# The second sequence product as Strassen blocks, with the scores spread over four pieces per pair of tiles

## The chip, the cores and the metric

The kernel runs on one core of one Trainium2 chip. The metric is the device time of one execution in microseconds (us), taken as the median of several runs. In the profile the core's engines are PE (TensorE, matrix products; PEld is its weight load), DVE (VectorE), ACT (ScalarE), POOL (GpSimd) and SP (SyncE, which issues DMAs). Each engine works through its own queue in order; an instruction that waits holds up all that stands behind it on that engine.

## The reference

```
g = sigmoid((x * gate_w).sum(-1))                  # x: 2048 x 640
a = x @ dft_hid_re.T ;  b = x @ dft_hid_im.T
A = dft_seq_re @ a - dft_seq_im @ b                # dft_seq_*: 2048 x 2048
q = x @ w_q                                        # 32 heads, 2 x 128 each
s1, s2 = q1 @ k1.T, q2 @ k2.T                      # 16 + 16 scores per head
top 2 of each, the 4 sums, top 2 of those -> 2 of 256 experts, softmax weights
B = sum over heads and picks of weight * gelu(x @ u[e]) * v[e]
y = g * A + (1 - g) * B
```

Everything is fp32, and the indices of the top picks need nearly full precision in the scores.

## The kernel before

The order of the products is turned round: first x^T C^T for C = dft_seq_re, then for C = dft_seq_im, and the hidden transforms last. Every fp32 product is three fp32r matmuls (`mm3`, L114 to L116: high part times high, high times low, low times high). The operand is split by `split` (L109 and L110): ACT copies the high part, and POOL or DVE subtracts it to get the low part.

**Pieces.** A sequence product runs over pieces, 128 in all: product w (0 for re, 1 for im), chunk c of 512 columns t (4 of them), tile s of 128 rows (16). `seq_piece(n)` loads the C tile of piece n+5 (SP's queue), splits the tile of piece n+3 (ACT, and POOL for the low part) and issues `mm3` into five accumulation banks, one for each tile d of 128 of the 640 columns of x. The x tiles X[0..15] stay in SBUF, split. After 16 pieces ACT copies the five banks out (tile `po`) and they go to `pd` in DRAM.

**Work between pieces.** `at(n, f)` hangs a step f on piece n, and `follow(n)` issues it there. Pieces 0 to 30 carry the folding of w_q with the keys. Then each pair of tiles of x gets its scores over five pieces: four halves of 512 scores (`score_half`: 5 `mm3` each) and the products with u (`u_pair`), so that the scores of the 16 tiles end with piece 70.

**The Pump.** Work of DVE without a due piece is a set of generators in `bg`: `topk` (10 operations on 128x1024 for each tile of x), `gates` (for each four tiles, weights and indices), `rows` (PE transposes of these, spaced out by a clock), and `experts` (last in order). `run_bg(us)` is called after each `mm3` with the PE time that it stands for; it adds share*us to a credit and issues generator steps while the credit lasts. All that is issued stands in the engines' queues in that order.

**Experts.** For each half g of the tokens, `experts(g)` goes over 16 chunks: DVE builds one-hot tiles pt and qt (three 128x1024 operations, L494 to L496), PE multiplies them (16 small matmuls of 64 columns, L516, into one of two PSUM banks), DVE masks and sums the result into `cd` (L501 and L503). The half's `cd` goes to DRAM (`gd`), from which the final product takes it.

**Final product.** For each chunk c of 512 tokens, `prepare(c)` loads the ten [128, 512] tiles of pd and the two of the experts' sums, DVE multiplies the gate in (L597, L614, L615), ACT makes the high parts, POOL or DVE the low ones. `y_tile(c, j)` then makes the five tiles j of the output from twelve `mm3` each, against the split DFT matrices of the hidden dimension (DD) and v (xh, xl). DD and v are loaded and split on POOL during pieces 74 to 89. `prepare(0)` runs one term for each piece from piece 113 on. After chunk 1, `bg.drain()` issues what is left.

Of the kernel before, what the change touches and what calls it, by code (L numbers as in the profile page):

```python
# [8 lines left out]
F32 = mybir.dt.float32  # L9
# [19 lines left out]
NPC = 2 * NC * NT  # L29
# [5 lines left out]
FAR = -3.0e38  # L35


class Pump:
# [41 lines left out]
    def drain(self):  # L80
        while (c := self.one()) is not None:
            assert c >= 0
# [3 lines left out]
def gated_mix_kernel(ctx: ExitStack, tc: tile.TileContext, xT, xn, dreT, dimT, wsre, wsim, wq, kT, uT, vv, gw, out):  # L86
# [8 lines left out]
    def bank():  # L95
        return psum.tile([P, TC], F32, name="pc", tag="pc", bufs=5)

    def ps_s(shape=(P, TC)):
        return psum.tile(list(shape), F32, name="pss", tag="pss", bufs=2)

    def ps_t(shape, dt=F32):
        return psum.tile(shape, dt, name="pst", tag="pst", bufs=1)

    def stage(name):
        return big.tile([P, TC], F32, name=name, tag="stg", bufs=5)
# [6 lines left out]
    def mm3(o, wh, wl, ah, al, first, last):  # L112

        nc.tensor.matmul(o, wh, ah, start=first, stop=False)  # L114
        nc.tensor.matmul(o, wh, al, start=False, stop=False)  # L115
        nc.tensor.matmul(o, wl, ah, start=False, stop=last)  # L116
# [5 lines left out]
    bg = Pump()  # L122

    def run_bg(us):
        bg.run(us, 0.95 if p3 is None else 1.0)


    WU = big.tile([P, 2 * KD * (HH * E + NE)], F32R, name="WU", tag="WU")
    NW = KD * HH * E
    WH, WL = (WU[:, n * NW:(n + 1) * NW].rearrange("p (k c) -> p k c", k=KD) for n in range(2))  # L130
    UH, UL = (WU[:, 2 * NW + n * KD * NE:2 * NW + (n + 1) * KD * NE].rearrange("p (k c) -> p k c", k=KD)
              for n in range(2))
# [3 lines left out]


    pieces = [(w, c, s) for w in range(2) for c in range(NC) for s in range(NT)]
    pf, psp, X, xr = {}, {}, {}, {}

    def load_piece(n):
        if n < NPC:
            w, c, s = pieces[n]
            pf[n] = big.tile([P, TC], F32, name="wf", tag="wf", bufs=5)
            nc.sync.dma_start(pf[n], (wsre, wsim)[w][c, s])

    def split_piece(n):
        if n < NPC:
            h = big.tile([P, TC], F32R, name="wh", tag="wh", bufs=4)
            l = big.tile([P, TC], F32R, name="wl", tag="wl", bufs=4)  # L150
            split(pf.pop(n), h, l, nc.gpsimd)
            psp[n] = (h, l)
# [4 lines left out]
    def seq_piece(n):  # L157
        w, c, s = pieces[n]
        if s == 0:
            banks[:] = [bank() for _ in range(KD)]  # L160
# [3 lines left out]
        for d in range(KD):  # L164
            ds = slice(d * P, (d + 1) * P)
            mm3(banks[d], X[s][:, 0, ds], X[s][:, 1, ds], h, l, s == 0, s == NT - 1)
            if s == NT - 1:
                f = stage("po")
                nc.scalar.activation(f, banks[d], AF.Copy)  # L169
                nc.scalar.dma_start(pd[w, c, d], f)  # L170
            run_bg(0.68)


    p1_stack = ctx.enter_context(ExitStack())
    p1 = p1_stack.enter_context(tc.tile_pool(name="p1", bufs=1, reuse_waits="tile"))

# [27 lines left out]
    warm = big.tile([P, 4 * P], F16, name="warm", tag="wl", bufs=4)  # L204
# [56 lines left out]
    def w_transposes(G, k0, k1):  # L261
# [4 lines left out]
        h = WH[:, k0:k1, P * G:P * (G + 1)]  # L266
        nc.scalar.activation(h, t[:, :k1 - k0], AF.Copy)  # L267
        nc.vector.tensor_sub(WL[:, k0:k1, P * G:P * (G + 1)], t[:, :k1 - k0], h.bitcast(F32))  # L268
# [11 lines left out]
    xf, xs = {}, {}  # L280

    def load_xT(p):
        if p < NP:
            xf[p] = big.tile([P, 2, KD, P], F32, name="xf", tag="xf")
            for n in range(2):
                nc.sync.dma_start(xf[p][:, n], xT[2 * p + n])

    def split_xT(p):
        if p < NP:
            xs[p] = tuple(big.tile([P, 2, KD, P], F32R, name=t, tag=t) for t in ("xh", "xl"))  # L290
            f = xf.pop(p)
            for n in range(2):
                split(f[:, n], xs[p][0][:, n], xs[p][1][:, n], nc.gpsimd)
            load_xT(p + 1)


    then = {}

    def at(n, f, *args):
        then.setdefault(n, []).append(lambda: f(*args))  # L300

    def follow(n):
        for f in then.pop(n, ()):
            f()
# [14 lines left out]
    at(n - 8, load_xT, 0)  # L319
    for k in range(KD):  # L320
        at(n - 8 + k, load_u, k)
        at(n - 6 + k, split_u, k)
    at(n - 3, split_xT, 0)
    N0 = n + 1
# [23 lines left out]
    def score_half(i, a):  # L348
        xh, xl = (t[:, i % 2] for t in xs[i // 2])
# [5 lines left out]
        c = slice(a * TC, (a + 1) * TC)  # L355
        for k in range(KD):
            mm3(ps, xh[:, k, :], xl[:, k, :], WH[:, k, c], WL[:, k, c], k == 0, k == KD - 1)
            run_bg(0.68)
        nc.scalar.activation(scs[i].rearrange("p h e -> p (h e)")[:, c], ps, AF.Copy)  # L359
# [66 lines left out]
    def rows(b):  # L426
# [11 lines left out]
        for ib in range(NB):  # L438
            bg.space(lambda ib=ib: row_tile(ib), 4.0 if ib else 12.0)
# [15 lines left out]
    def u_pair(p):  # L455
        xh, xl = xs.pop(p)
# [6 lines left out]
        act = stage("act").rearrange("p (n t) -> p n t", n=2)  # L463
# [4 lines left out]
    for p in range(NP):  # L468
        n = N0 + 5 * p
        for a in range(4):  # L470
            at(n + 1 + a, score_half, 2 * p + a // 2, a % 2)
        at(n + 4, u_pair, p)
        at(n + 4, split_xT, p + 1)
    N1 = N0 + 5 * NP

    def experts(g):
# [7 lines left out]
        def build(c):  # L486
# [7 lines left out]
            nc.vector.tensor_tensor(pt, row(0), wt, op=OP.is_equal)  # L494
            nc.vector.tensor_tensor(qt, row(1), wt, op=OP.is_equal)
            nc.vector.tensor_tensor(pt, pt, row(2), op=OP.mult)  # L496
# [231 lines left out]
```

## Time and profile before

| what | us |
| --- | --- |
| median of 3 runs (lowest, highest) | 812.57 (810.55, 814.08) |
| the profiled execution, its own time | 812.46 |
| its span in the profile | 810.7 |
| PE busy in it | 798.8 (99%) |
| DVE busy | 471.9 (58%) |
| POOL busy | 278.4 (34%) |
| ACT busy | 248.8 (31%) |
| mean granted TensorE clock | 0.996 |

The span is the profiled part of an execution; 1.8 us lie around it. A group of the profile is named by line, engine and operation, with output and inputs; the line is often a helper's (L110 is every low part). Matmuls overlap in the array, so the mean time of one (about 390 ns for 512 columns) is longer than the distance between two starts.

### The profile page before, as it was taken

How to read it: one execution, taken by the hardware profiler on the slowest of the kernel's cores; microseconds unless marked ns; L12 is line 12 of the kernel's file. 1: busy time of each engine (PE TensorE's matmuls, PEld its weight loads, DVE VectorE, ACT ScalarE, POOL GpSimd, SP SyncE). 2: the span in 40 equal slices, each digit the busy share in tenths (PEclk: the TensorE clock that was granted, in tenths of full speed). 3: DMA queues.
4: the chain of work that ended last, by engine and by line, in shares of the span. 5: the costliest groups of instructions: out<-in, count | busy, mean ns of one | idle time of the engine just before them, and what ended most of it. 6: DMA issues, size and time to landing. Idle time of an engine off the chain costs nothing.

```text
span 810.7 us, 10711 instructions
## 1 busy us (share of the span) xinstructions
PE 798.8 (99%) x4227; PEld 636.3 (78%) x4227; DVE 471.9 (58%) x561; ACT 248.8 (31%) x388; POOL 278.4 (34%) x192
## 2 busy tenths in 40 slices
PE   8999999999999999999998999999999999999998
PEld 5676667888888888888786777777777888888886
DVE  4841001086886898687688199776679743334200
ACT  3433323331217125224513722311322332222200
POOL 5433124224414153242424595343346222212000
PEclk9999999999999999999998999999999999999999
DMA  9877995402115030233212632423443274434101
GB/s 345 313 273 262 238 329 169 145 13 98 66 46 176 6 105 21 90 98 117 86 56 76 208 121 65 131 76 120 154 133 119 79 233 145 140 116 144 66 26 40
DMA packets 56002, 106.31 MB, mean 131 GB/s; under 512 B 8208, under 2 KB 15248, under 8 KB 55696
## 3 DMA queue, kind: packets, MB, share of 16 engines
q1 hardware_dynamic: 42944, 87.92, 33.6%
q10 hardware_dynamic: 13008, 17.71, 6.1%
q8 instruction: 33, 0.54, 0.3%
q14 instruction: 17, 0.14, 0.1%
HBM read 85.67 MB, written 19.93 MB: 130 GB/s over the span
## 4 chain that ended last, share of the span: by engine, by line
PE 90%; DMA 4%; DVE 3%; ACT 2%; SPq 0%; ACTq 0%; issue 0%; DVEq 0%
PE pc L114 24%; PE pc L116 22%; PE pc L115 22%; PE pss L114 6%; PE pss L116 6%; PE pss L115 6%; PE pss L253 2%; DMA wq<-in_wq 2%; PE pss L516 1%; DMA xr<-in_xn 1%; DMA wf<-in_wsre 1%; ACT po L169 1%; ACT rows L435 1%; PE pst L265 0%; ACTq L170 0%; DVE rp L412 0%
## 5 line engine op out<-in xcount | busy, mean ns | idle before, releaser
L110 POOL TENSOR_TENSOR wl<-wf,wh 128x512 fp32r<-128x512 f32 x128 | 187.4, 1469 | 281.3 <-ACT wh L109 266.1
L114 PE MATMUL pc<-wh,X 128*128 128x512 f32 x640 | 258.2, 404 | 0.4 <-ACT X L109 0.3
L115 PE MATMUL pc<-wl,X 128*128 128x512 f32 x640 | 251.0, 392 | 0.9 <-POOL wl L110 0.9
L116 PE MATMUL pc<-wh,X 128*128 128x512 f32 x640 | 251.1, 392 | 0.5 <-DVE X L110 0.3
L114 PEld LDWEIGHTS pc<-wh,X 128*128 128x128 f32 x640 | 120.9, 189 | 35.3 <-issue 8.1
L116 PEld LDWEIGHTS pc<-wh,X 128*128 128x128 f32 x640 | 120.7, 189 | 27.4 <-DVE X L110 1.3
L115 PEld LDWEIGHTS pc<-wl,X 128*128 128x128 f32 x640 | 121.0, 189 | 24.7 <-POOL wl L110 1.7
L109 ACT ACTIVATE wh<-wf 128x512 fp32r<-128x512 f32 x128 | 81.0, 633 | 130.4 <-PE pc L116 86.3
L373 DVE TENSOR_REDUCE mm<-sc 128x64 f32<-128x1024 f32 x32 | 39.0, 1220 | 67.7 <-ACT sc L359 67.2
L114 PE MATMUL pss<-WU,xh 128*128 128x512 f32 x160 | 62.5, 391 | 0.0
L116 PE MATMUL pss<-WU,xl 128*128 128x512 f32 x160 | 62.3, 389 | 0.0
L115 PE MATMUL pss<-WU,xh 128*128 128x512 f32 x160 | 62.3, 389 | 0.0
L114 PE MATMUL pc<-pz,DD 128*128 128x512 f32 x160 | 62.3, 389 | 0.0
L116 PE MATMUL pc<-pz,DD 128*128 128x512 f32 x160 | 62.2, 389 | 0.0
L115 PE MATMUL pc<-pz,DD 128*128 128x512 f32 x160 | 62.2, 389 | 0.0
L110 POOL TENSOR_TENSOR pz<-pr,pz 128x512 fp32r<-128x512 f32 x19 | 27.1, 1427 | 98.0 <-ACT pz L109 84.7
L110 POOL TENSOR_TENSOR xl<-xf,xh 128x640 fp32r<-128x640 f32 x16 | 32.9, 2079 | 75.4 <-ACT xh L109 75.4
L359 ACT ACTIVATE sc<-pss 128x512 f32<-128x512 f32 x32 | 21.1, 658 | 113.1 <-PE pss L116 112.7
L375 DVE TENSOR_TENSOR eq<-sc,mm 128x1024 f16<-128x1024 f32 x32 | 45.8, 1430 | 1.1
L109 ACT ACTIVATE pz<-pr 128x512 fp32r<-128x512 f32 x32 | 19.9, 631 | 78.5 <-DVE pr L597 50.4
L268 DVE TENSOR_TENSOR WU<-pst,WU 128x512 fp32r<-128x512 f32 (+1 forms) x16 | 7.8, 490 | 61.8 <-ACT WU L267 61.6
L501 DVE TENSOR_TENSOR tmp<-pss,mask 128x512 f32<-128x512 f32 x32 | 22.0, 689 | 34.6 <-PE pss L516 34.5
(112 smaller groups left out, 1066.3 us busy)
## 6 DMA issues: line engine op xcount, KB each, us to landing
wq<-in_wq SPq DMA_DIRECT2D x32, 640.0 KB, 6.2
wf<-in_wsre SPq DMA_DIRECT2D x64, 256.0 KB, 5.3
wf<-in_wsim SPq DMA_DIRECT2D x64, 256.0 KB, 2.9
pd<-po ACTq DMA_DIRECT2D x40, 256.0 KB, 3.6
pr<-pd SPq DMA_DIRECT2D x40, 256.0 KB, 3.3
xr<-in_xn SPq DMA_DIRECT2D x16, 320.0 KB, 6.2
xf<-in_xT SPq DMA_DIRECT2D x16, 320.0 KB, 3.3
out_y<-yo ACTq DMA_DIRECT2D x19, 256.0 KB, 2.4
```

The lines of the kernel that those rows point to most:

```text
L109: nc.scalar.activation(h, f, AF.Copy)
L110: eng.tensor_sub(l, f, h.bitcast(F32))
L114: nc.tensor.matmul(o, wh, ah, start=first, stop=False)
L115: nc.tensor.matmul(o, wh, al, start=False, stop=False)
L116: nc.tensor.matmul(o, wl, ah, start=False, stop=last)
L169: nc.scalar.activation(f, banks[d], AF.Copy)
L253: nc.tensor.matmul(ps[32 * j:32 * j + 32, :HALF], kp[:, 8 * G // H, r, :], w[:, j], start=(r == 0), stop=(r == 1))
L359: nc.scalar.activation(scs[i].rearrange("p h e -> p (h e)")[:, c], ps, AF.Copy)
L373: nc.vector.tensor_reduce(m, sc, op=OP.max, axis=AX.X)
L375: nc.vector.tensor_tensor(eq, sc, m[:, :, None].to_broadcast([P, HH, E]), op=OP.is_equal)
L435: nc.scalar.activation(ROWS[i // 8][:, :, :, i % 8], t, AF.Copy)
L501: nc.vector.tensor_tensor(tmp, t.rearrange("p m (e t) -> p (m e) t", t=4), mask4[:, None, :].to_broadcast([P, 8 * E, 4]), op=OP.mult)
```

## The change

The first product (C = dft_seq_re, 64 pieces) stays. The scores of a pair take four pieces instead of five, with `u_pair` beside the third half, and begin two pieces earlier (piece 30), so that they end with piece 61.

The second product is cut into four blocks: a half `sub` of the 16 tiles s (8 tiles) by a pair `tp` of the four chunks t. In a block, four of the five d tiles form a 2x2 matrix of halves, as do the tiles s (4 + 4) and the chunks (1 + 1), and the product of the 2x2 matrices takes seven products of halves instead of eight (the Winograd form of Strassen's step). The fifth d tile is done the plain way, in a bank of its own (W). A block has 28 steps: seven units (`UNITS`) by four tiles k. Units a11, a12, s1 and a22 issue three `mm3` for each k (two d tiles, and the fifth), units s2, s4 and s3 issue two: 72 in a block, 288 in all, where the 64 pieces before had 320.

What the seven products need and give:

- sums of C tiles: `add_a` (L215) adds a tile from DRAM onto one in SBUF by an accumulating DMA, issued on POOL's queue, four for each block (two tiles each); `add_s` (L220) is a DVE addition, eight for each block;
- sums of x tiles: `make_sums(sub, k)`, four times before each pair of blocks (from block 0's steps 0, 2, 4, 6 for the first half of s, from block 1's last step on for the second): 5 additions and 2 low parts on DVE, 4 high parts on ACT, 2 low parts on POOL;
- the C tiles as before, split at three steps ahead: 28 for each block, 16 low parts on POOL and 12 on DVE;
- results: after each unit `post` copies two banks by ACT (L336) or adds two banks to the copies by DVE (L340), with eight such additions for each block; `put` writes to pd, plainly on ACT's queue (L324) for the blocks of the first half of s, and by accumulating DMA on POOL's queue (L322) for the second.

Slots of SBUF and PSUM are shared by stage (tags W0 to W3, F0 to F2, WS, ST, SR; PSUM banks by number). DD and v are split on POOL in blocks 2 and 3 (`split_m`, 12 of 128x640) instead of right after the scores. In the final product all low parts are made on POOL, and the order of banks is a list (LAST).

The experts' one-hot products use a single bank (7), and their sums are one ACT copy (L732) and three DVE operations in a chain (L734). The Pump's share is 0.95 up to the blocks, 0.65 or 0.2 inside them, by the unit, and 0.95 after. `load_z(c)` first drains the Pump until the half of the experts that it needs is summed; in the final product that falls into the fifth y_tile of chunk 1.

```diff
+PAIR = 2 * TC
+NSTEP = 28
...
-    def drain(self):
-        while (c := self.one()) is not None:
+    def drain(self, until=lambda: False):
+        while not until() and (c := self.one()) is not None:
...
+    UNITS = ("a11", "a12", "s1", "s2", "s4", "a22", "s3")
+    def add_a(b, what, k2, row, col):
+        nc.gpsimd.dma_start(home[what, k2], src(b, row, col, k2), accum_op=OP.add)
+    def add_s(what, k):
+        f = home["s", k // 2][:, k % 2]
+        nc.vector.tensor_add(f, f, home[what, k // 2][:, k % 2])
+    def split_step(m):
...
+        split(home[key][:, k % 2], *sp[m], nc.vector if what in ("s2", "s3", "s4") else nc.gpsimd)
+    def make_sums(sub, k):
...
+        nc.vector.tensor_sub(t[:, :4 * P].rearrange("p (n d) -> p n d", n=2), f[:, :, 0:2 * P], f[:, :, 2 * P:4 * P])
+        nc.vector.scalar_tensor_tensor(t3, t1, -1.0, b22, op0=OP.mult, op1=OP.subtract)
+        nc.vector.tensor_sub(t5, t1, t5)
...
+        split(t[:, :8 * P].rearrange("p (n d) -> p n d", n=4)[:, 0:3:2], h, l, nc.gpsimd)
+        split(t5, t_sum(k, 2, 0), t_sum(k, 2, 1), nc.gpsimd)
+        nc.vector.tensor_sub(t6f, b22, b12)
+        nc.vector.tensor_sub(t5d, f[:, 1, 4 * P:], f[:, 0, 4 * P:])
+        split(t6f, t6(sub, k, 0), t6(sub, k, 1), nc.vector)
+        split(t5d, x5d(sub, k, 0), x5d(sub, k, 1), nc.vector)
+    def step(m):
...
+        if m + 3 < 4 * NSTEP:
+            split_step(m + 3)
...
+        for d in range(2):
+            mm3(roles[o][d], w(0)[:, c], w(1)[:, c], h, l, first and k == 0, k == 3, not first)
+            run_bg(0.68)
+        if w5:
+            mm3(roles["W"], w5(0), w5(1), h, l, ...)
+            run_bg(0.68)
+    def put(b, row, d, f):
...
+        if sub:
+            nc.gpsimd.dma_start(o, f, accum_op=OP.add)
+        else:
+            nc.scalar.dma_start(o, f)
...
-        bg.space(lambda ib=ib: row_tile(ib), 4.0 if ib else 12.0)
+        bg.space(lambda ib=ib: row_tile(ib), 4.0 if ib else 20.0 if b == NT // NB - 1 else 12.0)
...
-        n = N0 + 5 * p
+        n = N0 + 4 * p
...
+        at(NPC + 2 * k, make_sums, 0, k)
+        at(NPC + NSTEP + 27 + 2 * k, make_sums, 1, k)
...
         def sums(c, t):
-            nc.vector.tensor_tensor(tmp, ... mask4 ..., op=OP.mult)
-            nc.vector.tensor_reduce(cd[...], ..., op=OP.add, axis=AX.X)
+            nc.scalar.activation(o, t[:, :, :, 0], AF.Copy, scale=mask4[:, 0:1])
+            for n in range(1, 4):
+                nc.vector.scalar_tensor_tensor(o, t[:, :, :, n], mask4[:, n:n + 1], o, op0=OP.mult, op1=OP.add)
...
     def split_p(c, w, k):
-        split(f, *ops[c, w, k], nc.vector if k % 2 else nc.gpsimd)
+        split(f, *ops[c, w, k], nc.gpsimd)
     def load_z(c, k):
+        g = c // 2
+        bg.drain(lambda: g in summed)
```

Three places show how instructions now stand. The first is DVE's queue at the end of the scores. Names: `rr`, `mm`, `cc`, `pk` belong to topk and gates of the last tiles, `rp` to what PE transposes for `rows`. Before:

```order
L379 TENSOR_REDUCE rr<-eq 128x64
L392 TENSOR_TENSOR cc<-mm 128x128
L393 TENSOR_TENSOR cc<-mm 128x128
L394 TENSOR_TENSOR cc<-mm 128x128
L396 TENSOR_TENSOR pk<-cc 128x128
L397 TENSOR_TENSOR cc<-cc 128x128
L398 TENSOR_TENSOR cc<-cc 128x128
L403 COPY rp<-rr 128x4x32
L404 COPY rp<-rr 128x4x32
```

After, in the same place (`tf` is the scratch of make_sums, `rx` the x tiles it reads):

```order
L574 TENSOR_TENSOR cc<-cc 128x128
L575 TENSOR_TENSOR cc<-cc 128x128
L260 TENSOR_TENSOR tf<-rx_2962 128x512
L261 SCALAR_TENSOR_TENSOR tf<-tf,rx_2962 128x256
L262 TENSOR_TENSOR tf<-tf 128x256
L267 TENSOR_TENSOR tf<-rx_2962 128x256
L268 TENSOR_TENSOR tf<-rx_2962 128x128
L124 TENSOR_TENSOR X<-tf,X 128x256
L124 TENSOR_TENSOR X<-tf,X 128x128
L580 COPY rp<-rr 128x4x32
L581 COPY rp<-rr 128x4x32
```

One whole make_sums has moved in between the two halves of the last `gates`; two others stand ahead of the last topk operation shown.

The second place is POOL's queue at the end of block 1 and the start of block 2. `WS<-F`, `WS<-pf` and `WS<-SR` are low parts of C tiles, `tw` those of make_sums. Before, at about this place in the second product, POOL held the low parts of the C tiles and of DD:

```order
L110 TENSOR_TENSOR DD<-draw,DD 128x640
L110 TENSOR_TENSOR wl<-wf,wh 128x512 x5
L110 TENSOR_TENSOR xl<-draw,xh 128x640
L110 TENSOR_TENSOR wl<-wf,wh 128x512
L110 TENSOR_TENSOR xl<-draw,xh 128x640
L110 TENSOR_TENSOR wl<-wf,wh 128x512 x25
```

After:

```order
L124 TENSOR_TENSOR tw_3015<-tf,tw_3015 128x2x256
L124 TENSOR_TENSOR tw_3015<-tf,tw_3015 128x256
L215 DMA SR<-in_wsim 128x2x512
L124 TENSOR_TENSOR WS<-F_68,WS 128x512
L124 TENSOR_TENSOR WS<-F_69,WS 128x512
L124 TENSOR_TENSOR tw_3015<-tf,tw_3015 128x2x256
L124 TENSOR_TENSOR tw_3016<-tf,tw_3016 128x256
L215 DMA SR<-in_wsim 128x2x512
L124 TENSOR_TENSOR WS<-F_69,WS 128x512
L124 TENSOR_TENSOR WS<-pf,WS 128x512
L124 TENSOR_TENSOR tw_3016<-tf,tw_3016 128x2x256
L124 TENSOR_TENSOR tw_3017<-tf,tw_3017 128x256
```

Between every two low parts of C tiles there now stand two of make_sums, and the accumulating DMAs.

The third place is DVE's queue where chunk 1 of the final product ends. `pt` and `qt` are the one-hot tiles, `b_...` is the PSUM bank of their product. Before, the last experts stood among the preparation of a chunk (`za`, `zf`, `pz`):

```order
L496 TENSOR_TENSOR pt<-pt,rows_1258 128x1024
L614 TENSOR_TENSOR za<-za,zf 128x512
L615 TENSOR_TENSOR zf<-za,gm 128x512
L110 TENSOR_TENSOR pz<-zf,pz 128x512
L501 TENSOR_TENSOR tmp<-pss,mask_150 128x512
L503 TENSOR_REDUCE cd<-tmp 128x8x16
```

After, behind the last gate multiply (L810):

```order
L810 SCALAR_TENSOR_TENSOR F_70<-F_70,df 128x512
L734 SCALAR_TENSOR_TENSOR cd<-b_5735,mask_149,cd 128x8x16 x3
L721 TENSOR_TENSOR pt<-rows_1140,wtab_147 128x1024
L723 TENSOR_TENSOR qt<-rows_1140,wtab_147 128x1024
L725 TENSOR_TENSOR pt<-pt,rows_1140 128x1024
L734 SCALAR_TENSOR_TENSOR cd<-b_5782,mask_149,cd 128x8x16 x3
L721 TENSOR_TENSOR pt<-rows_1140,wtab_147 128x1024
L723 TENSOR_TENSOR qt<-rows_1140,wtab_147 128x1024
L725 TENSOR_TENSOR pt<-pt,rows_1140 128x1024
L734 SCALAR_TENSOR_TENSOR cd<-b_5808,mask_149,cd 128x8x16 x3
```

The last chunks of the experts now follow each other with nothing between; on PE the four one-hot products of chunks 12 to 15 of the second half stand back to back, with no `mm3` between them.

458 lines of the change are left out of this document (300 added, 158 removed).

## The prediction

> **What bounds the kernel now.** I read the page's busy shares and its chain of waits first, then the list of waits, then PE's timeline where the chain leaves PE.
>
> ```profile
> PE 798.8 (99%) x4227; PEld 636.3 (78%) x4227; DVE 471.9 (58%) x561; ACT 248.8 (31%) x388; POOL 278.4 (34%) x192
> PE 90%; DMA 4%; DVE 3%; ACT 2%; SPq 0%; ACTq 0%; issue 0%; DVEq 0%
> POOL wl L110 <- ACT wh L109: 273.6, 86, 10.2
> ACT wh L109 <- PE pc L116: 86.3, 30, 4.0
> ```
>
> PE is the bound: 99% busy, 90% of the chain. The last two rows (line that waited, for what, total us, times, longest) say that splits are made as soon as PE frees a slot: ACT waits for PE, POOL for ACT, and PE for neither. So every matmul taken away shortens the end, as long as the other queues keep their lead, and DVE's 58% is a mean over stages that differ. PE's own gap, at the last row transposes:
>
> ```profile
> 434.27 0.39 PE L114 MATMUL pc<-wh,X 128*128 128x512 f32 x1
> ...
> 435.41 0.39 PE L116 MATMUL pc<-wh,X 128*128 128x512 f32 x1
> ...
> 440.27 0.29 PE L434 MATMUL pst<-ident,gs 128*128 128x128 f16 x1 [2.34 <-DVE gs L422]
> 440.32 0.78 PE L114 MATMUL pc<-wh,X 128*128 128x512 f32 x1
> 440.90 0.63 PE L115 MATMUL pc<-wl,X 128*128 128x512 f32 x1
> ...
> 445.59 0.51 PE L114 MATMUL pc<-wh,X 128*128 128x512 f32 x1
> 445.94 0.40 PE L115 MATMUL pc<-wl,X 128*128 128x512 f32 x1
> 417.93 0.60 ACT L359 ACTIVATE sc<-pss 128x512 f32<-128x512 f32 x1 [5.68 <-PE pss L116]
> 429.79 1.22 DVE L379 TENSOR_REDUCE rr<-eq 128x64 f16<-128x1024 f16 x1
> 439.79 0.43 DVE L422 TENSOR_TENSOR gs<-cc,gs 128x256 f16<-128x256 f32 x1
> ```
>
> Warm, five starts from 434.27 to 435.41 are 0.228 us apart, so one `mm3` is 0.68. Then PE stands for 4.9 us, until DVE has done the last topk and gates (22.3 us from the score copy at 417.93 to 440.27). After it matmuls start 0.43 apart: 13 take 5.62 us where 2.96 would do, 2.7 lost to the cold clock.
>
> **The change, part by part.**
>
> *Matmuls removed.* 320 `mm3` of the second product become 288: 96 matmuls by 0.228 = **−21.9**. No row bounds this from another side; it comes in full wherever PE is not made to wait.
>
> *Scores over four pieces.* A pair of tiles takes 34.2 us of PE now: five pieces of 3.42, 20 `mm3` of scores (13.7), and `u_pair` with 10 of half the width (3.4). With one piece less it is 30.8.
>
> ```profile
> 345.00:385.00 40.00, 40.00 (x205) 34.02 (x204) 33.29 (x45) 13.94 (x22) 12.77 (x7) 1.00 0.33 109
> 464.00:484.00 20.00, 20.00 (x143) 15.56 (x143) 18.77 (x15) 6.83 (x11) 18.88 (x11) 1.00 0.45 146
> 500.00:520.00 20.00, 20.00 (x143) 15.59 (x142) 15.02 (x21) 3.77 (x7) 7.13 (x6) 1.00 0.25 68
> ```
>
> The windows' columns are length, then busy PE, PEld, DVE, ACT and POOL. In the first, in the scores, DVE has 33.3 of 40 us, or 28.5 a pair: 92% of 30.8. It still fits: **0**, at most 0.5; without that cover each us beyond 30.8 would cost one, for each of eight pairs.
>
> *Contention.* The second window (DD being split) has DVE at 94% and POOL at 94% with 15 DVE operations; the third has 21 in 15.0 us. The rows:
>
> ```profile
> 477.14 1.74 POOL L110 TENSOR_TENSOR wl<-wf,wh 128x512 fp32r<-128x512 f32 x1
> 507.70 1.29 POOL L110 TENSOR_TENSOR wl<-wf,wh 128x512 fp32r<-128x512 f32 x1 [1.90 <-ACT wh L109]
> 478.84 1.56 POOL L110 TENSOR_TENSOR DD<-draw,DD 128x640 fp32r<-128x640 f32 x1
> 478.97 1.98 DVE L494 TENSOR_TENSOR pt<-rows,wtab 128x1024 f16<-128x1024 f16 x1
> 480.88 1.77 DVE L495 TENSOR_TENSOR qt<-rows,wtab 128x1024 f16<-128x1024 f16 x1
> 509.47 0.68 DVE L495 TENSOR_TENSOR qt<-rows,wtab 128x1024 f16<-128x1024 f16 x1
> 510.07 0.68 DVE L496 TENSOR_TENSOR pt<-pt,rows 128x1024 f16<-128x1024 f16 x1
> ```
>
> A POOL subtraction takes 1.29 alone and 1.74 against DVE; a DVE one-hot operation 0.68 alone and 1.8 to 2.0 against POOL. One of each together costs 1.74. The changed blocks put more on both engines, so terms below lie between quiet and contended. [...]
>
> *Block 0, make_sums.* Its DVE part has no row. Nearest are these:
>
> ```profile
> L597 DVE SCALAR_TENSOR_TENSOR pr<-pr,grow x40: 676/684/1767, 595.5 to 759.9; 128x512 f32<-128x512 f32 x40
> L110 DVE TENSOR_TENSOR WU<-uf,WU 128x256 fp32r<-128x256 f32 x5 | 2.5, 490 | 7.2 <-ACT WU L109 7.2
> L392 DVE TENSOR_TENSOR cc<-mm 128x128 f32<-128x128 f32 x4 | 1.1, 283 | 0.0
> 502.16 0.44 PE L516 MATMUL pss<-qt,pt 128*64 128x64 f16 x16
> ```
>
> 0.68 + 4×0.49 + 2×0.28 = 3.2, less some overlap of starts: 3.0. Three of them now stand in DVE's queue ahead of the last gates: 22.3 + 9 = 31.3 from score copy to last transpose. PE has 33 `mm3` between, 22.5 us, where it had 17.5: the gap grows from 4.9 to 8.8, and make_sums also waits for its x tiles and for ACT and POOL to leave its single scratch: **+4.5**. Ends: 0, where DVE gets ahead in the four-piece scores; +9, where each make_sums runs contended. The cold part stays the same.
>
> *Start of block 2, make_sums again.* In eight steps of `mm3` triples (16.4 us of PE) POOL has eight chunk splits and four make_sums (one 128x512 and one 128x256 each, taken as 1.29 and 0.65) and two accumulating DMAs. Quiet: 10.3 + 7.8 = 18.1, plus the DMAs; contended, 1.74 and 0.87: 13.9 + 10.4 = 24.4. DVE has 12 of make_sums, 4 additions from PSUM and 4 of C tiles at 0.69, and builds at a share of 0.65 (10.6): 28 us. ACT's puts wait for DVE's PSUM additions. The splits' lead of three steps (6.1 us) absorbs the first part. Over by 2 to 12, less some lead: **+6.5**; ends 0 (the lead covers it) and 12. Next late: the low parts that s1 needs.
>
> *Blocks 1 and 3, and the short units.* The same work without make_sums, with 8 additions and up to 6 accumulating puts in POOL's queue, where each waits for DVE and holds the splits behind it: **+3.5**; ends 0 and 7. Accumulating DMAs on POOL have no row; the nearest transfers:
>
> ```profile
> wf<-in_wsim SPq DMA_DIRECT2D x64, 256.0 KB, 2.9
> pd<-po ACTq DMA_DIRECT2D x40, 256.0 KB, 3.6
> 2.11 0.43 SPq L145
> ```
>
> A quarter of a MB lands after 2.9 to 3.6 us and an issue is 0.43 on SP; I take POOL's issue at that, 0.4 to 0.9, and a double-sized accumulating load at two landings, 5.8 to 7.2. These loads start three steps (6.1 us) ahead of their first use, so they just arrive; the price if late is in the last case below.
>
> *First output chunk.* From step 20 of block 3 PE has 21.1 us up to the first `y_tile`, and POOL has twelve pz splits, two of 128x640 and four DMAs: 12×1.29 + 2×1.56 + 4×0.43 = 20.3 quiet, with the block's last splits about 25 contended: **+5**. Ends 0 and 9. Before, these low parts were halved between DVE and POOL over 15 pieces.
>
> *The drain.* In the fifth `y_tile` of chunk 1 four one-hot groups follow each other on PE. Each round waits for the sums of the group before (the single bank; ACT copy 0.3 to 0.4, three chained DVE operations, 0.9 by the 128x128 row) and mostly for its build (three by 0.6 = 1.8): first group at once, then 1.9, 2.7, 2.7 and the close, 7.9 in all, of which 4×0.44 is work that PE has anyway: 6.1 idle. Behind it stands the clock: if the gate closes, 2.7 more as after the row gap. The bursts of 0.44 leave PE mostly idle for longer than 4.9 us, so I take it as closed: **+8.7**; ends 6 and 12. [...]
>
> *Sum.* −21.9 + 0 + 4.5 + 6.5 + 3.5 + 5 + 8.7 = +6.3. On the span of 810.7 that is 817.0, and with the 1.8 around it 818.8 of the execution's own 812.46, which stands 0.1 below the median of 812.57: **819**. By the terms' ends the extremes are −15.4 and +28.1, 797 and 841.
>
> **The rivals.**
>
> *A: the lead covers the blocks.* POOL had 66% of the span free, and in the third window only 7.1 of 20 us; if its lead hides blocks 1 to 3 and the first chunk, only the row gap and the drain are paid: 812.5 − 21.9 + 4.5 + 8.7 = 803.8, or 801 with the clock kept. It speaks for this that low parts of the s units lie on DVE, so that POOL catches up there (8 of 28 steps without a POOL split in a row); against it, that DVE then has both. It decides if POOL's split plus make_sums stays under 4.1 us for two steps: quiet 4.5, with the lead enough.
>
> *B: DVE and POOL bound the blocks throughout.* As in the second window, where both stood at 94%. With builds at 1.8 to 2.0, one-hot work of 16 chunks adds some 3.5 us a chunk to DVE, and the DMA waits in POOL's queue keep the lead at zero: the block terms at their ends, 12 + 7 + 9, with 4.5 + 8.7: 812.5 − 21.9 + 41.2 = 832. Against it: the Pump's share of 0.65 or 0.2 throttles the builds.
>
> *C: accumulating loads arrive late.* Each block's sums need four; if each were 1.5 us late beyond the forecast, PE would lose 4 × 1.5 = 6: 825. A DMA that waits for POOL to issue it can show that; nothing in the trace of before does.
>
> **How the numbers follow.** Forecast 0.50 (own range 810 to 828, since the terms' ends hardly fall together), A 0.27, B 0.15, C 0.08. The bound of a difference that a measurement of this kernel can tell is 0.5%: 808.5 and 816.6. A gives faster in 0.24 and no change in 0.03; the forecast's own lower part gives 0.05 faster and 0.13 no change; the rest, with B and C, is slower: 0.55. The range goes from inside A to inside B, 799 to 836, leaving 2 in 10 out.
>
> **What would show it.** Matmuls of the second product: 864 where there were 960. PE's gap at the last row transposes: about 9 us. Idle PE at the start of block 2 with POOL's low parts as releaser: 4 to 9 us. Idle PE before the first y_tiles of chunk 0, released by POOL `pz`: about 5. Four one-hot groups some 2.7 apart in chunk 1, then starts 0.43 apart. Wrong if PE's idle time in the blocks sums to under 5 us (then A), or if DVE's windows there read over 95% throughout (then B); wrong in another way if single matmuls in the blocks start further apart than 0.23 with no wait shown.

## The result, and the profile after

The changed kernel takes 929.87 us (median of 4, 925.6 to 934.89) where the kernel before takes 812.0 beside it: ratio 1.145, interval 1.138 to 1.152. It is slower, as forecast, but by 118 us, not 6, and far above the range. The profiled execution has a span of 931.0. First the page's busy shares and its chain, then the largest rows of the list of what PE waited for (total us, times, longest):

```profile
PE 816.9 (88%) x4131; PEld 641.6 (69%) x4131; DVE 586.8 (63%) x741; ACT 308.4 (33%) x520; POOL 349.0 (37%) x260
PE 63%; DVE 13%; DMA 8%; issue 5%; POOL 5%; ACT 4%; SPq 1%; ACTq 1%; DVEq 0%; POOLq 0%
```

```profile
PE b L742 <- DVE cd L734: 46.3, 16, 5.5
PE b L129 <- POOL WS L124: 29.9, 11, 7.5
PE b L129 <- POOL pz L124: 9.5, 3, 7.8
PE b L610 <- DVE rp L589: 6.6, 1, 6.6
PE b L128 <- ACT WS L123: 6.6, 4, 3.6
...
PE b L611 <- DVE gs L599: 2.2, 1, 2.2
```

PE's share of the chain has gone from 90% to 63%: PE is no longer the bound. It stood idle for 106 us in the second half; the kernel before stood for 4 there. No single engine takes its place (DVE 63%, POOL 37%): the engines wait for each other. The largest row is the one-hot products of the experts (L742), which wait for the sums of the chunk before (L734); the kernel before has no wait ahead of any of its 32 groups of these. The next is the low parts of C tiles on POOL. The matmuls are as forecast: 96 fewer of 512 columns.

Then the clock. PE's timeline behind one such gap (the granted clock is 0.55 from 410 to 416 us, and 1.00 from 416 to 420):

```profile
410.23 0.80 PE L129 MATMUL b<-WS,X 128*128 128x512 f32 x1 [4.97 <-POOL WS L124]
410.82 0.63 PE L130 MATMUL b<-WS,X 128*128 128x512 f32 x1
411.25 0.63 PE L128 MATMUL b<-WS,X 128*128 128x512 f32 x1
```

Starts are 0.43 apart, not 0.23. Such starts number 139 in the second half, against 13 before: 139 × 0.2 = 28 us. So the balance is 812 − 21.9 (matmuls) + 102 (more idle) + 25 (more slow starts) = 917. The 13 that are left lie mostly at the edges of the gaps, where a start is further from the next than idle time and a slow start make it (0.59 from 410.23 to 410.82), and in one-hot groups that took 0.64 in place of 0.44.

**What POOL waited for.** POOL's timeline, at four of its DMAs:

```profile
622.28 1.24 POOL L215 DMA_DIRECT2D SR<-in_wsim  x1
628.43 1.21 POOL L322 DMA_DIRECT2D pd<-ST  x1 [3.60 <-issue]
634.83 1.22 POOL L322 DMA_DIRECT2D pd<-ST  x1 [5.18 <-issue]
640.95 1.22 POOL L215 DMA_DIRECT2D SR<-in_wsim  x1 [3.60 <-issue]
```

They come 6.1 to 6.4 us apart, idle time stands before each with no releaser shown ("issue"), and the median time to landing of these DMAs is 6.1. Each of the last three waited for the one before, of 512 KB, to land: by the trace the first three landed at 628.12, 634.51 and 640.61, and the next one started 0.31 to 0.34 us later each time. PE's wait that ended at 637.39 (7.5 us, for POOL's low part of 635.58) lies behind the one at 634.83.

**What DVE waited for.** The timelines of DVE and of POOL, near 690 us:

```profile
689.96 7.94 DVE L124 TENSOR_TENSOR WS<-F,WS 128x512 fp32r<-128x512 f32 x1 [1.21 <-ACT WS L123]
690.24 1.74 POOL L124 TENSOR_TENSOR WS<-F,WS 128x512 fp32r<-128x512 f32 x1
691.47 2.01 POOL L124 TENSOR_TENSOR d<-df,d 128x640 fp32r<-128x640 f32 x1
692.96 1.74 POOL L124 TENSOR_TENSOR WS<-F,WS 128x512 fp32r<-128x512 f32 x1
694.19 1.73 POOL L124 TENSOR_TENSOR pz<-SR,pz 128x512 fp32r<-128x512 f32 x1
695.41 1.75 POOL L124 TENSOR_TENSOR WS<-F,WS 128x512 fp32r<-128x512 f32 x1
```

An operation of DVE that took 0.69 at 495.54 took 7.94 here, while POOL ran five in a row.

**What the one-hot product waited for.** The timelines of DVE, ACT and PE around 495 us (L340 adds from PSUM, L732 and L734 are the sums):

```profile
493.11 1.27 DVE L340 TENSOR_TENSOR ST<-ST,b 128x512 f32<-128x512 f32 x2
494.88 0.63 ACT L123 ACTIVATE WS<-SR 128x512 fp32r<-128x512 f32 x1 [3.87 <-DVE ST L340]
495.41 0.47 ACT L732 ACTIVATE cd<-b,mask 128x128 f32<-128x128 f32 x1
495.54 0.69 DVE L124 TENSOR_TENSOR WS<-SR,WS 128x512 fp32r<-128x512 f32 x1 [1.16 <-ACT WS L123]
496.15 1.40 DVE L734 SCALAR_TENSOR_TENSOR cd<-b,mask,cd 128x128 f32<-128x128 f32 x3
497.60 0.64 PE L742 MATMUL b<-qt,pt 128*64 128x64 f16 x16 [4.21 <-DVE cd L734]
```

The product of the chunk before ran at 485.93. Its sums stand in the code behind the next chunk's build, so ACT reached L732 only at 495.41, behind a put that waited for DVE's addition; DVE did L734 at 496.15, and the next product, issued straight behind these sums, waited 4.2 us for the single bank. (The kernel before has two banks for it; no run gives the changed kernel its second bank back, so what the bank alone costs, wherever the sums stand, is not known.)

### The profile page after: what moved, and what is told of

The parts are those of the page before. It is cut to its first block, busy times and chain, and to the rows that moved or that the text cites. A ratio compares the mean times of both kernels' runs of the same rounds, so it can differ in the third digit from the quotient of the medians.

```text
span 931.0 us, 11018 instructions
## 1 busy us (share of the span) xinstructions
PE 816.9 (88%) x4131; PEld 641.6 (69%) x4131; DVE 586.8 (63%) x741; ACT 308.4 (33%) x520; POOL 349.0 (37%) x260
## 4 chain that ended last, share of the span: by engine, by line
PE 63%; DVE 13%; DMA 8%; issue 5%; POOL 5%; ACT 4%; SPq 1%; ACTq 1%; DVEq 0%; POOLq 0%
PE b L128 20%; PE b L129 19%; PE b L130 19%; DVE cd L734 3%; POOL WS L124 2%; PE b L441 2%; DMA wq<-in_wq 2%; DVE pt L725 1%; DMA SR<-pd 1%; POOL pz L124 1%; DMA SR<-gd 1%; DVE WS L124 1%; ACT WS L123 1%; DMA xr<-in_xn 1%; PE b L742 1%
## 5 line engine op out<-in xcount | busy, mean ns | idle before, releaser
L124 POOL TENSOR_TENSOR WS<-F,WS 128x512 fp32r<-128x512 f32 x104 | 157.5, 1546 | 205.6 <-ACT WS L123 204.2
L129 PE MATMUL b<-WS,X 128*128 128x512 f32 x504 | 204.7, 406 | 20.6 <-POOL WS L124 17.1
L128 PE MATMUL b<-WS,X 128*128 128x512 f32 x504 | 209.0, 415 | 8.4 <-ACT WS L123 6.6
L130 PE MATMUL b<-WS,X 128*128 128x512 f32 x504 | 203.6, 404 | 0.1
L129 PEld LDWEIGHTS b<-WS,X 128*128 128x128 f32 x504 | 99.0, 197 | 43.8 <-POOL WS L124 19.7
L128 PEld LDWEIGHTS b<-WS,X 128*128 128x128 f32 x504 | 99.0, 197 | 40.1 <-ACT WS L123 9.1
L130 PEld LDWEIGHTS b<-WS,X 128*128 128x128 f32 x504 | 98.5, 195 | 22.1 <-DVE X L124 0.6
L123 ACT ACTIVATE WS<-F 128x512 fp32r<-128x512 f32 x112 | 69.5, 625 | 68.0 <-PE b L130 31.3
L129 PE MATMUL b<-pz,d 128*128 128x512 f32 x200 | 81.0, 405 | 9.5 <-POOL pz L124 9.5
L128 PE MATMUL b<-pz,d 128*128 128x512 f32 x200 | 81.7, 409 | 1.0 <-ACT pz L123 1.0
L130 PE MATMUL b<-pz,d 128*128 128x512 f32 x200 | 80.4, 402 | 0.0
L734 DVE SCALAR_TENSOR_TENSOR cd<-b,mask,cd 128x128 f32<-128x128 f32 x96 | 43.8, 456 | 38.0 <-ACT cd L732 35.8
L128 PE MATMUL b<-W,xT 128*128 128x512 f32 x160 | 62.8, 392 | 0.0
L130 PE MATMUL b<-W,xT 128*128 128x512 f32 x160 | 62.3, 389 | 0.0
L129 PE MATMUL b<-W,xT 128*128 128x512 f32 x160 | 62.3, 389 | 0.0
L124 POOL TENSOR_TENSOR xT<-xT,xT 128x640 fp32r<-128x640 f32 x16 | 27.6, 1727 | 87.7 <-ACT xT L123 87.7
L742 PE MATMUL b<-qt,pt 128*64 128x64 f16 x512 | 16.2, 213 | 46.4 <-DVE cd L734 46.3
L124 POOL TENSOR_TENSOR pz<-SR,pz 128x512 fp32r<-128x512 f32 x25 | 35.2, 1437 | 56.1 <-ACT pz L123 56.1
L123 ACT ACTIVATE WS<-SR 128x512 fp32r<-128x512 f32 x56 | 35.4, 644 | 62.3 <-PE b L130 39.9
L742 PEld LDWEIGHTS <-pt 128*64 128x64 f16 x512 | 12.4, 125 | 58.3 <-DVE cd L734 52.7
L129 PE MATMUL b<-WS,tw 128*128 128x512 f32 x96 | 41.1, 429 | 12.7 <-POOL WS L124 12.7
```

The lines of the kernel that those rows point to most:

```text
L123: nc.scalar.activation(h, f, AF.Copy)
L124: eng.tensor_sub(l, f, h.bitcast(F32))
L128: nc.tensor.matmul(o, wh, ah, start=first, stop=False, skip_group_check=more)
L129: nc.tensor.matmul(o, wh, al, start=False, stop=False, skip_group_check=more)
L130: nc.tensor.matmul(o, wl, ah, start=False, stop=last, skip_group_check=more)
L734: nc.vector.scalar_tensor_tensor(o, t[:, :, :, n], mask4[:, n:n + 1], o, op0=OP.mult, op1=OP.add)
```

## The experiments

Four theories. S: the sums' place, just ahead of the next product, makes PE wait for the queues of ACT and DVE at each chunk. D: POOL's DMAs wait for each other and hold low parts behind them. P: DVE and POOL slow each other's operations down. M: the work of make_sums and of the other new low parts does not fit in the blocks.

**e1: sums straight behind their product.**

```diff
         yield from build(0)
         for c in range(16):
+            if c + 1 < 16:
+                yield from build(c + 1)
...
-            if c + 1 < 16:
-                yield from build(c + 1)
-            else:
-                yield 3.4
             sums(c, t)
```

> Order of the experts changed alone: chunk c+1 is built before the one-hot product of chunk c, and the sums of chunk c are issued straight behind that product, not just ahead of the next one (the single bank stays). Theory S (the sums stand in the queues of ACT and DVE just ahead of the next product, so PE waits for both queues at each chunk): PE's idle time before L742 falls from 46 us to under 12, and the time from 930 to 865 to 885. Theory D (POOL's accumulating DMAs hold the low parts behind them): the stalls come back at the low parts, 915 to 925. Theory P (DVE and POOL hinder each other in SBUF): as many operations as before on both, 915 to 930.

920.2 (ratio 1.131, 1.118 to 1.145): 9.7 less than the 929.9 of the changed kernel, a difference that the two intervals don't quite separate. S's time missed by 35; it lies in the ranges of D and of P. PE's waits in this run (an edit shifts the lines; L744 is the one-hot product, L742 above):

```profile
PE b L129 <- POOL WS L124: 42.5, 15, 9.7
PE b L744 <- DVE cd L734: 15.6, 5, 4.4
```

The wait for the sums fell from 46.3 to 15.6, but that for POOL rose from 29.9 to 42.5: a good part of the time only moved on.

**e2: no experts.** Their loop is replaced by `nc.vector.memset(cd, 0.0)`.

> The experts' builds, one-hot products and sums are left out (cd is set to zero, so the B part is missing). The products themselves are 14 us of PE. Theory S: 930 - 14 - 46 idle - some 20 of cold clock behind those stalls = about 850. Theory D: 930 - 14 and little more, 900 to 915. Theory P: 96 of the large DVE operations are gone, so POOL is no longer held: under 835, and PE's waits for POOL's low parts fall from 38 us to under 10.

871.1 (one run), in none of the three ranges. The experts cost the changed kernel 59 us, not the 14 of their products. PE still waited 40.1 us for POOL's low parts, so S doesn't explain those, and P's forecast, that they fall under 10 with the experts' DVE operations gone, failed too.

**e3: a larger scratch.**

```diff
-    nc = bacc.Bacc(..., dynamic_dma_scratch_size=1024)
+    nc = bacc.Bacc(..., dynamic_dma_scratch_size=2048)
-    warm = p1.tile([P, 4 * P], F16, name="warm")
+    warm = big.tile([P, 4 * P], F16, name="warm", tag="ST")
```

> The scratch for POOL-issued DMAs is 2048 bytes per partition, not 1024 (and the warm-up tile lies in another slot). Theory D, in the form that a POOL DMA waits until the one before it has landed, since the scratch holds one: the idle time of POOL before its DMAs that shows no releaser (34 us in 7 places) falls under 8, two DMAs come closer than 6.1 us, PE's waits for low parts fall from 38 to under 25, time 895 to 912. Theories S and P: 920 to 935, and the spacing of 6.1 stays if the scratch is not what it waits for.

896.0 (1.102, 1.095 to 1.108): 34 us less. POOL's DMAs at the same place of the code, and PE's waits:

```profile
607.00 1.22 POOL L215 DMA_DIRECT2D SR<-in_wsim  x1
609.02 2.92 POOL L322 DMA_DIRECT2D pd<-ST  x2
```

```profile
PE b L742 <- DVE cd L734: 43.1, 17, 5.4
PE b L129 <- POOL WS L124: 4.4, 5, 1.7
```

The idle time of POOL without a releaser (33.6 us in the changed kernel) is gone, a second DMA starts 2.0 us behind the first and a third right behind that, and PE's wait for low parts falls from 29.9 to 4.4, further than expected. D is shown, in this form: with 1024 bytes POOL's DMAs at this place started only 0.31 to 0.34 us after the one before had landed, and with 2048 the next one started 2.0 us behind the first, where landing had taken 5.8 to 6.1 in the changed kernel.

**e4: no DMA on POOL's queue.** `add_a` returns at once, and `put` uses ACT's queue for all blocks.

> No DMA on POOL's queue: the second addend of the sums of C tiles is not loaded, and the second half's results overwrite the first half's on ACT's queue (so the second product is not the reference's). Theory D: PE's waits for POOL's low parts fall from 38 us to under 12, time 885 to 900. Theory S: PE's idle time before L742 stays over 40, time 910 to 930. Theory P: 915 to 930.

871.9 (one run), below D's range and 24 less than with the larger scratch. PE's largest wait in this run (L739 is the one-hot product here):

```profile
PE b L739 <- DVE cd L731: 34.1, 14, 7.5
```

PE's waits for the C tiles' low parts on POOL are 3.5 us, against 4.4 in e3; those for the experts' sums are 34.1, against 43.1, and there are 54 slow starts, against 105. So what the scratch doesn't cure reached PE mostly through the sums. Whether it is the waiting of POOL's queue for what a DMA needs or the DMAs' own traffic was not told apart.

**e5: both edits, e1 and e3.**

> Both edits together: sums of a chunk straight behind its one-hot product, and 2048 bytes of scratch. Theory 'queues' (the two waits feed each other: with the ring gone, PE's 43 us before the one-hot products remain, and with the sums moved, PE's 41 us at the low parts remain): together PE's idle time in the second half falls from 106 to about 45, and the time to 845 to 865, more than the sum of the single gains (9.7 and 34). Theory 'one cause' (the sums' place costs only what the first edit alone gained): 880 to 890.

880.0 (1.083, 1.078 to 1.088). The theory of two waits that feed each other missed by 15, and the time lies in the range of the other: the sums' place is worth 16 with the larger scratch. PE's waits, and the windows of the columns named in the prediction, for 480 to 550 and 620 to 680:

```profile
PE b L129 <- POOL WS L124: 16.5, 17, 2.8
PE b L744 <- DVE cd L734: 16.5, 5, 5.3
```

```profile
480.00:550.00 70.00, 59.86 (x322) 44.04 (x322) 57.83 (x84) 26.95 (x54) 33.01 (x26) 0.98 0.65 185
620.00:680.00 60.00, 48.32 (x195) 35.23 (x195) 52.47 (x56) 22.12 (x40) 34.19 (x27) 0.83 0.73 185
```

The gaps are many and small now, and DVE is 83 to 87% busy in these windows.

**e6: the first of the four sums on DVE, not ACT**, on top of e5 (`nc.vector.tensor_scalar(o, t[:, :, :, 0], mask4[:, 0:1], None, op0=OP.mult)`).

> As the run before, and the first of the four sums is a DVE operation and not an ACT copy, so that the bank comes free without ACT's queue. If ACT's queue (its copies wait for slots that PE frees) is what still holds the sums: DVE's wait for ACT before L734 (43 us with the sums moved alone) is gone, and the time falls another 8 to 20 us, to 830 to 850. If DVE itself is late: equal within 5 us, since DVE gets 32 operations of 0.3 more.

886.9 (1.091, 1.085 to 1.098). It isn't 8 to 20 less; that it is 7 more is not settled, since the interval overlaps that of e5. PE's wait for the sums is as long as in e5, though no copy by ACT stands ahead of them any more:

```profile
PE b L744 <- DVE cd L734: 16.2, 5, 4.2
```

So ACT's copy isn't what is late; the wait is for DVE.

**e7: on top of e6, low parts of the final product alternate, and the rows come later.**

```diff
+        last = b == NT // NB - 1
+        if last:
+            bg.clock = 0.0
         for ib in range(NB):
-            bg.space(lambda ib=ib: row_tile(ib), 4.0 if ib else 20.0 if b == NT // NB - 1 else 12.0)
+            bg.space(lambda ib=ib: row_tile(ib), 4.0 if ib else 10.0 if last else 12.0)
...
-        bg.credit -= 0.7
+        bg.credit -= 1.4 if k % 2 else 0.7
         ops[c, w, k] = slot()
-        split(f, *ops[c, w, k], nc.gpsimd)
+        split(f, *ops[c, w, k], nc.vector if k % 2 else nc.gpsimd)
```

> As the run before, and the low parts of the final product's tiles alternate between DVE and POOL (as in the kernel before), and the last row transposes stand 10 us later on PE. PE's idle time before the first pz (5 to 9 us) and before the row transposes (7.5 to 8.9 us) goes, with 2.7 of cold clock behind each: 12 to 20 us less than the run before, 815 to 835. If DVE is then the late one, PE waits for DVE's low parts instead and the gain is under 8.

894.3 (1.100, 1.096 to 1.105), far above both forecasts, and 14 above e5; against e6 the intervals overlap. PE's wait at the rows is gone, but the experts start later (their first product at 468.0 us, not 462.8), and PE's waits for their sums grew from 16.2 in e6 to 26.5, five groups of the drain among them. The work was moved to where DVE had no time for it either.

**e8: the rows later in the kernel before** (the same edit there, with 7.0).

> The kernel before, with its last row transposes 7 us later on PE (the clock of their spacing is set back when they are queued). If the stall of 4.9 us and the 2.7 us of cold clock behind it are a matter of where the transposes stand: 804 to 807, ratio 0.990 to 0.994. If the experts, which then start later, run out of time before the final product: 811 to 816.

807.7 (0.9959, 0.9935 to 0.9983): faster by a little, just short of the first range. PE still waits 1.6 us there for the gates.

**e9 and e10: no experts, in the changed kernel with the larger scratch, and in the kernel before.**

> The changed kernel without the experts' builds, products and sums (the B part is missing) and with 2048 bytes of scratch. With 39 us of PE waiting for POOL in the run without experts and 27 of slow or missing starts: if the scratch alone made those waits, they fall under 6 and the time from 871 to 822 to 838. If POOL is late for another reason as well (DVE's splits and additions hold it in SBUF): 845 to 860.

> The kernel before without the experts' builds, products and sums (the B part is missing). Its PE loses 32 groups of 0.44: 812 - 14 = 797 to 800 if the experts cost nothing beside their products; less if they hold PE elsewhere. The run before minus this one is what the Strassen blocks cost without experts and without the scratch's waits: -22 + stalls.

832.6 and 794.7. The first lies in the range of the scratch alone, but its condition fails: PE still waits 14.1 us for the C tiles' low parts on POOL and 5.3 for pz. The second is 2 below its range: the experts cost the kernel before 16 to 17 us. Without them and with the larger scratch the changed kernel is still 38 us behind, although it has 22 of matmuls less. Windows of e9, in block 0 (PE waits for ACT's high parts, 2.52 us of it up to 471.65, with the DMA share at 1.00; that ACT waited for a C tile's DMA is an estimate from these two), block 1, and block 2:

```profile
460.00:480.00 20.00, 15.03 (x43) 11.29 (x44) 5.27 (x9) 6.68 (x12) 8.32 (x7) 0.74 1.00 314
480.00:500.00 20.00, 20.00 (x90) 16.54 (x89) 6.77 (x11) 7.90 (x13) 9.32 (x8) 1.00 0.50 133
540.00:560.00 20.00, 16.08 (x66) 11.59 (x64) 19.05 (x22) 11.07 (x23) 15.05 (x13) 1.00 0.41 83
```

In block 1 PE doesn't wait at all. In block 2, with make_sums, DVE is 95% and POOL 75% busy, and PE waits.

These runs take the 118 us apart. The larger scratch is worth 34 (929.9 to 896.0). The experts then cost 63 (896.0 to 832.6), where they cost the kernel before 17 (812.0 to 794.7): 46 more. The 38 that are left are the blocks without experts. The experts' 46 is the largest part, and the runs explain only some of it: the sums' place is 16 (e5).

**e11: a share of 0.95 in the blocks**, on top of e5.

> Sums behind their product and 2048 bytes of scratch (880), and the Pump's share stays 0.95 in the blocks. If DVE is overfull in the blocks, each expert step put there delays the additions and low parts that PE needs: 885 to 905, though the drain in the final product (7.6 us idle in three gaps) goes. If DVE had room and only the drain costs: 862 to 874.

902.8 (1.112, 1.106 to 1.118): 23 more, as the first theory had it. DVE has no room in the blocks: it is 97% busy in block 2.

**e12: all low parts of C tiles in the blocks on DVE**, on top of e5.

> Sums behind their product and 2048 bytes of scratch (880), and DVE makes all low parts of the C tiles in the blocks, not 12 of 28. Theory P (each POOL subtraction holds DVE, one DVE operation of 0.69 lasted 7.9 while POOL ran five): DVE gets 64 operations of 0.69, 44 us, but its operations no longer last 1.1 to 1.4 on average: 850 to 872. If DVE's load alone decides: 890 to 925, with DVE over 95% busy in the blocks.

870.8 (1.073, 1.063 to 1.082): in P's range, and not more but perhaps 9 less (the interval overlaps that of e5 a little), although DVE has 64 operations more. DVE's groups of one-hot builds from 395 to 760 us, of e5 and then of this run:

```profile
L725 DVE TENSOR_TENSOR pt<-pt,rows 128x1024 f16<-128x1024 f16 x28 | 38.0, 1359 | 0.0
L721 DVE TENSOR_TENSOR pt<-rows,wtab 128x1024 f16<-128x1024 f16 x28 | 34.8, 1242 | 0.0
```

```profile
L725 DVE TENSOR_TENSOR pt<-pt,rows 128x1024 f16<-128x1024 f16 x29 | 23.1, 797 | 0.0
L721 DVE TENSOR_TENSOR pt<-rows,wtab 128x1024 f16<-128x1024 f16 x29 | 21.2, 733 | 0.0
```

The same builds fall from 1.36 and 1.24 us to 0.80 and 0.73 where POOL has no subtractions of C tiles. P is shown, with its price: over the whole kernel DVE is busy for 579.3 us with 805 operations, where in e5 it was busy for 593.4 with 741. POOL's 64 subtractions cost DVE more than doing them itself.

**e13 to e15: what is left of make_sums, of split_m and of the final product's low parts**, all from e9 (no experts, 2048 bytes). e13 leaves out the second half's make_sums and the loads of the x tiles for them, e14 gives split_m's low parts to DVE, e15 does both and alternates the final product's low parts.

> As the run without experts and with 2048 bytes of scratch (832.6), and the second half's make_sums are left out (its blocks multiply the sums of the first half: wrong data, the same matmuls). If they are what makes blocks 2 and 3 late: PE's idle time between 520 and 565 us (9 us in six gaps) goes, 818 to 826. If POOL is late there for the other low parts as well: 828 to 833.

> As the run without experts and with 2048 bytes of scratch (832.6), and the twelve low parts of 128x640 (DD and v) in blocks 2 and 3 are made by DVE, which is 40 to 60% idle there without experts. If these hold the C tiles' low parts behind them on POOL (12 x 1.8 us): PE's idle time from 570 to 660 falls from 11 to under 5, 820 to 827. If not: 830 to 835.

> Both edits, and the low parts of the final product's tiles alternate between DVE and POOL as in the kernel before. If the three together are the rest: stalls are left only at the row transposes (7 us, 5 in the kernel before) and in block 0, and the time is 800 to 812, some 10 above 794.7 - 22 + 23. If another cause is left (transfers that come late for ACT: 9 us of PE waiting for ACT's high parts): 815 to 825.

821.9, 829.2 and 812.7 from 832.6: make_sums of the second half cost 10.7, split_m on POOL some 3 (its two runs lie 8.5 apart, so that is not settled), all three edits together 20, so M holds for about half of the 38. At 812.7, 40 us are still left above 794.7 − 22. PE's list there has 30 us of waits, the largest these:

```profile
PE b L128 <- ACT WS L123: 8.3, 5, 2.5
PE b L129 <- POOL WS L124: 7.5, 9, 1.8
PE b L610 <- DVE rp L589: 4.7, 1, 4.7
```

In e10, which the 40 are counted from, PE is idle for 6 and has 10 slow starts. So e15 has 24 us more idle and, with its 47 slow starts, 7 more of those: 31 of the 40, and the rest is at the edges of the gaps. Of the 30 us of waits 17.7 lie in block 0 (6.9 at the row transposes), 6.9 in block 3 and 5.3 in the final product.

**e16: the rows 9 us later in the kernel before.**

> The kernel before with its last row transposes 9 us later, not 7 (807.7). The 1.6 us that PE still waits for gates at 443.5 go: 804.5 to 807, ratio 0.991 to 0.995. If the wait only moves with the queues: 807 to 809.

806.1 (0.9933, 0.9908 to 0.9959), in the first range. PE's timeline at the transposes has no wait left:

```profile
443.31 0.29 PE L433 MATMUL pst<-ident,rp 128*128 128x128 f16 x2
443.44 0.22 PE L434 MATMUL pst<-ident,gs 128*128 128x128 f16 x1
```

This is faster than both kernels: the one long stall of the kernel before, 4.9 us and its slow starts, was worth 5.8 us.

## Why the prediction was wrong

*Right: the sign, the matmuls and the row gap.* Ahead of the last row transposes PE's waits were 0.69 + 0.99 + 2.34 = 4.0 in the kernel before and 6.6 + 2.2 = 8.8 after: 4.8 more, where +4.5 was forecast.

*Right in kind, too small.* The drain, forecast at 8.7 with rounds of 2.7, shows four products 3.1 apart with 2.2 to 2.7 idle before each (the first was not "at once"), 9.9 together, and ten slow starts behind them, 2.0 more: just at the upper end of 12. The granted clock in the window of 820 to 840 us was 0.66 (last column but two). PE's timeline and that window:

```profile
823.97 0.44 PE L742 MATMUL b<-qt,pt 128*64 128x64 f16 x16 [2.25 <-DVE cd L734]
827.08 0.64 PE L742 MATMUL b<-qt,pt 128*64 128x64 f16 x16 [2.67 <-DVE cd L734]
830.19 0.64 PE L742 MATMUL b<-qt,pt 128*64 128x64 f16 x16 [2.48 <-DVE cd L734]
833.30 0.64 PE L742 MATMUL b<-qt,pt 128*64 128x64 f16 x16 [2.47 <-DVE cd L734]
```

```profile
820.00:840.00 20.00, 10.13 (x89) 7.83 (x88) 13.03 (x26) 4.75 (x9) 3.80 (x3) 0.66 0.17 48
```

The first output chunk, +5 with ends 0 and 9, showed 9.5 us of waits for pz, 4.8 with the larger scratch. The start of block 2, +6.5 with ends 0 and 12, measured 10.7 in e13, without the experts. In the changed kernel itself its sign, 4 to 9 us with POOL's low parts as releaser, did not come: in block 2 (538 to 621 us) PE waited 1.4 for those, and 18.6 for the experts' sums.

*Failed: "Accumulating DMAs on POOL have no row", and "I take POOL's issue at that, 0.4 to 0.9".* The bound was taken from SP's queue, which didn't wait for its own transfers (in the kernel before a load issued at 184.46 landed 2.7 us later, and the next was issued at 184.84). In the changed kernel a POOL DMA took 0.9 to 1.7 to issue, and behind one of 512 KB it also waited for that one to land; with the larger scratch the kernel is 34 us faster (e3). Case C named late loads, priced at 6 and given 0.08, but not that everything behind them on POOL waits too. The term that had these puts in it, +3.5 for blocks 1 and 3, was the most under-sized: in these blocks (470 to 538 and 621 to 714 us) PE was idle for 40 us, 21.5 of it for POOL's low parts of C tiles; with the larger scratch it was 21 and 0.7.

*Failed: the single bank was priced at one place.* The prediction saw that each one-hot product waits for the sums of the one before, and charged it only in the drain. The same order of instructions holds in every chunk: the 16 gaps before L742 come to 46.3 us, of which the drain has 9.9 and the blocks have 27.4. Had the rule been applied to each chunk whose sums stand just ahead of the next product, the term would have had some 36 us of waits more. Not all of that is time: moving the sums gave 9.7 alone and 16 with the larger scratch.

*Failed: "One of each together costs 1.74".* That was the alternation of the kernel before, one POOL operation to one of DVE. In the changed kernel POOL ran five subtractions in a row from 690.24 on, and one of DVE's lasted 7.94 beside them, against the 1.74 of a pair. By which mechanism POOL's operations lengthen DVE's was not shown.

*Failed: the cold clock was charged at two gaps.* With many gaps of 2 to 8 us it came to 139 slow starts, 28 us in place of 5.4. The prediction's one case of it was the row gap of the kernel before, 4.9 us of idle time with a granted clock of 0.51 behind it (440 to 446 us), and it took the drain as slow because PE would be idle there for longer; of the gate that it speaks of, the runs show the granted clock and the distance of starts alone. The trace has slow starts behind shorter gaps too: eleven behind a single one of 2.80 (granted clock 0.50 from 611 to 616 us), and ten behind the drain's series of 2.2 to 2.7.

```profile
610.68 0.64 PE L742 MATMUL b<-qt,pt 128*64 128x64 f16 x16 [2.80 <-DVE cd L734]
...
611.84 0.63 PE L129 MATMUL b<-WS,x5b 128*128 128x512 f32 x1
612.27 0.63 PE L130 MATMUL b<-WS,x5b 128*128 128x512 f32 x1
```

Two sums of the prediction are off without changing the outcome. The ends of the terms add up to −15.9 and +27.6, not −15.4 and +28.1. And the 21.1 us "up to the first `y_tile`" are 31 `mm3`; from step 20 on block 3 has 20, which is 13.6.

So rival B came nearest: waits for DVE and POOL in all blocks, with a price (41 us) of under a third of the real one (118 + 22 = 140). Its sign did not come: DVE was busy for 59 to 82% of each block, not over 95%. The terms were added as if each queue were late once. The engines wait for each other in a circle: ACT's put for DVE's addition, DVE for ACT's copy and for POOL, POOL for its DMA, PE for all three. A delay taken out of one came back in the others, as in e1, where 31 us taken from one wait gave some 10 in time; that this circle, and nothing else, makes the sum of the parts is argued, not shown.

What stays open: some 30 us of what the experts cost (46 less the 16 of the sums' place), to which DVE's longer operations beside POOL's belong in a part that e12 doesn't give; the 24 us between e3 and e4; and the split of e15's last 40 between late C tiles, POOL's low parts and the row gap.

## What to carry to other kernels

Matmuls saved on the bounding engine are worth their time only as long as the others keep their lead; here 22 us of them bought work for DVE and POOL in stages where these had little room, and cost 140. When an order such as "the reader of a bank stands just ahead of its next writer" is found at one place, count every place where the code has it. Before a DMA goes on an engine that also computes, bound what the queue behind it loses if the DMA must wait, not only its issue.

## What the runs showed of the hardware

- With 1024 bytes of scratch, three DMAs of POOL that each stood behind one of 512 KB started 0.31 to 0.34 us after that one had landed (628.43, 634.83 and 640.95 in the changed kernel; 5.8 to 6.1 us to land). Behind one of 256 KB, issued at 576.32 and landed 4.3 us later, the next started at 578.17. With 2048 bytes (e3) a second one started 2.0 us behind the first, and the kernel was 34 us faster.
- In the changed kernel a DVE subtraction at 689.96 took 7.94 us, one of the same shape at 495.54 took 0.69; beside the first, five of POOL's started 1.2 to 1.5 apart. 128x1024 builds fell from 1.2 to 1.4 us (e5) to 0.7 to 0.8 (e12) when POOL's subtractions of C tiles were taken away.
- In the changed kernel a single idle gap of 2.80 us on PE, up to 610.68, was followed by eleven matmul starts 0.43 apart, not 0.23, with a granted clock of 0.50 from 611 to 616 us.
